# The last chunk's output stores: from GpSimd's queue to the queues of SyncE and ScalarE

## The chip, the cores and the metric

The kernel runs on one core of one Trainium2 chip. The metric is the device time of one execution in microseconds, as the median of several runs. Before the change it is 883.96 us (three runs, 883.19 to 884.87). The profile is one execution, with a span of 881.4 us from its first to its last instruction.

## The reference

A bucketed attention feeds a two-layer block with a squared ReLU:

```python
# q, k, v: (4, 8, 768, 64); proj: (64, 6)
mask   = bucket(q @ proj)[..., :, None] == bucket(k @ proj)[..., None, :]
scores = where(mask, q @ k.T / 8, -1e9)
attn   = softmax(scores)                      # + 1e-9 in the sum
x = (attn @ v).transpose(0, 2, 1, 3).reshape(3072, 512)
h = x @ w_in                                  # (512, 2048)
g = relu(h) ** 2
out = g @ w_out                               # (2048, 512) -> (3072, 512), float32
```

The change concerns only how the last part of `out` leaves the chip.

## The kernel before, in words

The first part, about 0.4 of the span, computes the attention for 16 pairs of heads and keeps the transposed result `x_all` in DRAM. The second part works through the 3072 tokens in three chunks of NCH = 1024. For each chunk it makes the hidden layer (`hidden` for the first chunk, `hidden_pair` for the others) and then projects it (`project(i)`). The products are done with a two-level scheme of seven products instead of eight: `project` goes through seven outer products k = 0 to 6, and each of these is one call of `product`, which does seven inner ones.

`product` (L696) is the piece to know. It makes seven `add`s of four matmuls each (128x256, float32; each shows as two records in the trace), always in the order of factors 0, 1, 4, 3, 5, 6, 2. Adds of factors 0, 4, 5 and 2 go one after another into the same PSUM accumulator `acc0`, and after each of the first three ScalarE takes a snapshot of it (`keep`, L715: the copies `one`, `two`, `three`). The copy has to read the accumulator before the next add changes it, so TensorE waits for `one` before the add of factor 4, for `two` before that of factor 5, and so on. Between adds of `acc0` stand adds into another accumulator, which give the copy time.

Weights come as `leaf` tiles of 256 KB, seven buffers in rotation. Each add calls `a_with_load` (L1136), which issues the load of the leaf five places ahead on ScalarE's queue (`load_leaf`, L988). So ScalarE's instruction stream is a mixture of copies and of leaf loads, in the order of the program.

VectorE combines the products into blocks of the output. A finished block (i, ih, jh) of 128 output columns by 512 tokens goes to `put_out` (L1014): VectorE transposes it within 32x32 squares into a tile `h` (L1018), and four stores write it, one for each group of 32 partitions, a = 0 to 3 (L1025). Each moves 64 KB in runs of 128 bytes. Here ih says which half of the 512 output columns it is, jh which half of the chunk's tokens. Blocks (0,0), (0,1) and (1,0) go out on SyncE's queue (SP), blocks (1,1) on GpSimd's. In the last chunk (i = 2) the first (1,0) block alternates between SP and GpSimd.

Outer product k = 5 (`sixth`, L1097) closes the blocks (0,1) and (1,1), two rows of each; k = 6 (`fourth`, L1105) closes (1,0). The second (1,0) block of the last chunk, the very last output, is handled by `put_last` (L1030): TensorE transposes, ScalarE and VectorE copy one half each (L1040, L1042), and SP and ScalarE store them (L1045).

Each engine carries out its instructions in the order in which the program is built. Stores and loads on ScalarE's queue are issued by ScalarE's sequencer between its copies. After `project` of the last chunk all engines read a flag and pass over a general version of the kernel that is not used for these inputs (L1278, L1279).

The calls around the change are these:

```python
use = uses[k]                     # k = 5: sixth, k = 6: fourth
product(
    NQ, QN, a_with_load, bt, lambda *p: use(0, *p), lambda *p: use(1, *p),
    lambda p: use(2, p, None), lambda *p: use(3, *p), hook,
)
```

so that the blocks of n = 1 (row 0) are closed after the sixth add of a product and those of n = 2 (row 1) after its seventh, and the stores stand at these places of the program, before the first `add` of the next product.

Of the kernel before, what the change touches and what calls it, by code (L numbers as in the profile page):

```python
# [34 lines left out]
def kernel(  # L35
# [10 lines left out]
    nc = tc.nc  # L46
# [20 lines left out]
    NCHUNK = B * S // NCH  # L67
# [516 lines left out]
    with tc.manual_schedule():  # L584
# [21 lines left out]
        for pr in range(NP):  # L606
            a, b = 2 * pr, 2 * pr + 1
# [406 lines left out]
        def put_out(i, ih, jh, n, o):  # L1014


            ot = p_r.tile([P, HN], FP32, name="h", bufs=NH)
            nc.vector.transpose(out=ot, in_=o)  # L1018
            m0 = ih * HD + n * P
            at = slice(i * NCH + jh * HN, i * NCH + (jh + 1) * HN)  # L1020
            for a in range(P // 32):
                queue = nc.gpsimd if (ih, jh) == (1, 1) else nc.sync
                if (i, ih, jh) == (NCHUNK - 1, 1, 0) and a % 2:
                    queue = nc.gpsimd
                queue.dma_start(  # L1025
                    out=out[at, m0 + a * 32:m0 + (a + 1) * 32].rearrange("(c i) j -> i c j", i=32),
                    in_=ot[a * 32:(a + 1) * 32].rearrange("i (c j) -> i c j", j=32),
                )
# [21 lines left out]
        def project(i):  # L1050
# [12 lines left out]
            def close(ih, jh, n):  # L1063
                o = outs[ih, jh, n // 2]
                o[1] += 1
                if (i, ih, jh, n // 2) == (NCHUNK - 1, 1, 0, 1):

                    if o[1] == 2:
                        for col in (1, 0):
                            put_last(n - n % 2 + col, o[0][:, col * QN:(col + 1) * QN])  # L1070
                elif o[1] == 2:
                    put_out(i, ih, jh, n // 2, o[0])
# [407 lines left out]
```

## Time and profile before

| what | value |
|---|---|
| time, median of 3 | 883.96 us (883.19 to 884.87) |
| span of the profiled run | 881.4 us |
| TensorE busy | 866.7 us, 98% |
| VectorE busy | 756.3 us, 86% |
| ScalarE busy | 391.9 us, 44% |
| GpSimd busy | 107.2 us, 12% |
| chain that ended last | 94% TensorE |
| stores of L1025 on SP | 66, of 64 KB |
| stores of L1025 on GpSimd | 26, of 64 KB; 10 of them in the last 20 us |

In the views, PE is TensorE's matmuls and PEld its weight loads, DVE is VectorE, ACT ScalarE, POOL GpSimd and SP SyncE; SPq and ACTq are transfers as the engine's sequencer issues them. A line of the timeline gives the start, the length, the engine, the line of the kernel, the operation, the tile written and the tile read, the count of merged instructions, and in brackets the idle time of the engine before it with what ended it. A line of the chain gives start, length and what the time was spent in. An issue's length is the time on the issuing sequencer and not that of the transfer; the landing times are told apart.

### The profile page before, as it was taken

The numbers are of one execution on the slowest core, as the hardware profiler recorded it, in microseconds if no ns is written. First come the engines' busy times: TensorE is split into PE (matmuls) and PEld (weight loads), VectorE is DVE, ScalarE is ACT, GpSimd is POOL, SyncE is SP. The second block draws the span as 40 slices with busy tenths as digits, with TensorE's granted clock in tenths as the row PEclk, the third lists the DMA queues.
The fourth block names the chain that finished last, engine by engine and source line by source line (L and its number), as shares of the span: only waits on it lengthen the run. The fifth ranks groups of instructions, "written<-read, shape, count | busy, mean of one in ns | idle before, by whom it ended". The sixth has DMA issues, their size and how long they took to land.

```text
span 881.4 us, 12164 instructions
## 1 busy us (share of the span) xinstructions
PE 866.7 (98%) x4364; PEld 519.5 (59%) x4364; DVE 756.3 (86%) x1096; ACT 391.9 (44%) x673; POOL 107.2 (12%) x172
## 2 busy tenths in 40 slices
PE   8999999999999999999999999999999999999996
PEld 3444444444444444444688875556888755568885
DVE  5899999999999998888779978888889788888875
ACT  5988878888888861222211123332111233321110
POOL 2000000000000000564222021111100211110002
PEclk9999999999999999999999999999999999999999
DMA  9678779889677545989897675436847744454565
GB/s 184 123 152 136 196 180 193 178 278 212 148 167 188 156 150 172 322 258 290 282 352 252 181 163 172 159 116 230 291 144 185 174 156 157 129 167 149 162 173 105
DMA packets 224131, 167.09 MB, mean 190 GB/s; under 512 B 164448, under 2 KB 181344, under 8 KB 224064
## 3 DMA queue, kind: packets, MB, share of 16 engines
q1 hardware_dynamic: 189152, 87.19, 41.0%
q0 software_dynamic: 12528, 41.30, 14.9%
q10 hardware_dynamic: 22384, 37.76, 14.1%
q8 instruction: 36, 0.59, 0.3%
q14 instruction: 31, 0.25, 0.1%
HBM read 124.52 MB, written 41.68 MB: 189 GB/s over the span
## 4 chain that ended last, share of the span: by engine, by line
PE 94%; DVE 2%; ACT 1%; DMA 1%; issue 1%; ACTq 0%; DVEq 0%
PE acc L708 40%; PE st L396 17%; PE acc L927 16%; PE xo L438 13%; PE acc L880 5%; PE tot L457 2%; PE hash L346 1%; DVE total L428 1%; DMA k_nat<-in_k_dram 1%; ACT e L413 1%; ACT bits L356 1%; DMA w_in<-s_in 0%; DVE out_piece L179 0%; DVE power L171 0%; ACT small L160 0%
## 5 line engine op out<-in xcount | busy, mean ns | idle before, releaser
L413 ACT ACTIVATE e<-st 128x1024 f32<-128x1024 f32 x192 | 145.1, 810 | 46.9 <-PE st L396 42.7
L396 PE MATMUL st<-feat,feat 64*128 64x512 f32 (+1 forms) x768 | 150.4, 483 | 0.0
L438 PE MATMUL xo<-e,v_nat 128*64 128x512 f32 (+1 forms) x768 | 134.8, 492 | 0.0
L708 PE MATMUL acc<-b,leaf 128*128 128x256 f32 x600 | 133.4, 379 | 0.6 <-issue 0.6
L708 PEld LDWEIGHTS acc<-b,leaf 128*128 128x128 f32 x600 | 113.8, 190 | 17.3 <-issue 2.0
L428 DVE TENSOR_TENSOR total<-total,e 128x1536 f32<-128x1536 f32 x61 | 107.1, 1756 | 4.4
L438 PEld LDWEIGHTS xo<-e,v_nat 128*64 128x64 f32 x768 | 51.4, 136 | 82.4 <-issue 74.9
L927 PE MATMUL acc<-t_x,w_unit 128*128 128x512 f32 x192 | 90.2, 592 | 0.0
L396 PEld LDWEIGHTS st<-feat,feat 64*128 64x128 f32 x768 | 66.0, 188 | 33.5 <-issue 24.1
L708 PE MATMUL acc<-t,leaf 128*128 128x256 f32 x336 | 76.2, 380 | 0.0
L356 ACT ACTIVATE bits<-hash,lifts 32x384 bf16<-32x384 f32 x120 | 68.7, 573 | 3.2 <-issue 1.3
L708 PEld LDWEIGHTS acc<-t,leaf 128*128 128x128 f32 x336 | 63.7, 190 | 9.1 <-DVE t L519 0.5
L792 DVE SCALAR_TENSOR_TENSOR b<-h 128x512 f32<-128x512 f32 x96 | 65.7, 692 | 3.0
L396 PE MATMUL st<-bits,bits 64*128 64x256 bf16 (+1 forms) x384 | 63.0, 325 | 1.8 <-ACT e L413 1.4
L927 PE MATMUL acc<-x,w_unit 128*128 128x512 f32 x128 | 60.1, 592 | 0.0
L708 PE MATMUL acc<-x,w_unit 128*128 128x512 f32 x128 | 56.6, 594 | 0.0
L708 PE MATMUL acc<-b_t,leaf 128*128 128x256 f32 x240 | 53.8, 379 | 0.0
L927 PEld LDWEIGHTS acc<-t_x,w_unit 128*128 128x128 f32 x192 | 36.5, 190 | 28.9 <-issue 26.8
L715 ACT COPY two<-acc 128x256 f32<-128x256 f32 (+1 forms) x29 | 12.5, 432 | 87.7 <-PE acc L708 72.2
L715 ACT COPY one<-acc 128x256 f32<-128x256 f32 (+1 forms) x29 | 12.5, 432 | 85.9 <-PE acc L708 47.6
L708 PEld LDWEIGHTS acc<-b_t,leaf 128*128 128x128 f32 x240 | 45.5, 190 | 6.2
L396 PEld LDWEIGHTS <-bits 64*128 64x128 bf16 x384 | 23.4, 93 | 41.6 <-issue 37.9
(161 smaller groups left out, 1169.7 us busy)
## 6 DMA issues: line engine op xcount, KB each, us to landing
leaf<-w_out ACTq DMA_DIRECT2D x142, 256.0 KB, 3.1
w_unit<-w_in SPq DMA_DIRECT2D x16, 640.0 KB, 3.9
raw<-in_moe_w_in_dram SPq DMA_DIRECT2D x16, 512.0 KB, 5.5
raw<-in_moe_w_out_dram SPq DMA_DIRECT2D x16, 512.0 KB, 4.3
w_unit<-w_in SPq DMA_DIRECT2D x8, 896.0 KB, 7.9
w_out<-sums POOLq DMA_DIRECT2D x16, 448.0 KB, 6.8
sum<-w_in SPq DMA_DIRECT2D x16, 448.0 KB, 4.9
v_nat<-in_v_dram SPq DMA_DIRECT2D x16, 384.0 KB, 4.4
```

Of the source, the lines that this page charges most:

```text
L346: nc.tensor.matmul(out=banks[g * NR_B:(g + 1) * NR_B, h, 0:HS], lhsT=projs[rows], rhs=feat[pr, w][rows, c * HS:(c + 1) * HS], start=True, ...
L356: nc.scalar.activation(out=t[h * D:h * D + NR_B, c * HS:(c + 1) * HS], in_=hashed[pr, w][at, h, 0:HS], func=ACTF.Sign, scale=HUGE, bias=li ...
L396: nc.tensor.matmul(out=st[:, h, 0:hi - lo], lhsT=src[pr, 1][rows, key], rhs=src[pr, 0][rows, lo:hi], start=first, stop=not first,)
L413: nc.scalar.activation(out=e[:, :, lo:hi], in_=sts[i][:, :, 0:hi - lo], func=ACTF.Exp, scale=scale)
L428: nc.vector.tensor_tensor(out=totals[pr], in0=totals[pr], in1=weights[pr, kt][:, :, 0:S], op=ALU.add)
L438: nc.tensor.matmul(out=xo[h * D:(h + 1) * D, lo:hi], lhsT=nat[pr, "v_nat"][:, h, kt * D:(kt + 1) * D], rhs=weights[pr, kt][:, h, lo:hi], s ...
L457: nc.tensor.matmul(out=tot[g * 32:(g + 1) * 32, 0:HS], lhsT=ones, rhs=src[:, h, c * HS:(c + 1) * HS], start=src is srcs[0], stop=src is sr ...
L708: nc.tensor.matmul(out=acc[to], lhsT=a(i), rhs=b(i), start=first and i == 0, stop=last and i == n - 1, skip_group_check=True,)
L715: nc.scalar.copy(out=t, in_=acc[of])
L792: nc.vector.scalar_tensor_tensor(out=out, in0=h, scalar=0.0, in1=h, op0=ALU.max, op1=ALU.mult)
L880: nc.tensor.matmul(out=out, lhsT=w[:, a], rhs=b, start=start, stop=stop, skip_group_check=True)
L927: nc.tensor.matmul(out=acc[to], lhsT=w[:, PLACE[a], f], rhs=bt[b](f), start=first and f == 0, stop=last and f == NFT // 2 - 1, skip_group_ ...
```

## The change

In the last chunk no store is put on GpSimd's queue any more. The blocks of the lower half of the output columns (ih = 1), which are (1,1) and (1,0), alternate between SP and ScalarE: groups a = 0 and 2 on SP, a = 1 and 3 on ScalarE. It is meant to take GpSimd's slower issue out of the end of the kernel and to let two sequencers issue the last stores side by side. Chunks 0 and 1 stay as they were, and so does `put_last`.

```diff
             for a in range(P // 32):
                 queue = nc.gpsimd if (ih, jh) == (1, 1) else nc.sync
-                if (i, ih, jh) == (NCHUNK - 1, 1, 0) and a % 2:
-                    queue = nc.gpsimd
+
+                if i == NCHUNK - 1 and ih == 1:
+                    queue = (nc.sync, nc.scalar)[a % 2]
                 queue.dma_start(
                     out=out[at, m0 + a * 32:m0 + (a + 1) * 32].rearrange("(c i) j -> i c j", i=32),
                     in_=ot[a * 32:(a + 1) * 32].rearrange("i (c j) -> i c j", j=32),
                 )
```

## Prediction

> **What bounds the kernel now.** The page's parts 1 and 4 come first: TensorE is busy 98% of the span, and 94% of the chain that ended last is TensorE. The chain in order of time, cut to the last stretch, shows which engine sets the end, and where it stops doing so.
>
> ```profile
> 860.40 10.38 PE acc L708 x48
> 870.77 0.03 issue
> ...
> 871.79 0.71 DVE h L1018
> 872.50 0.32 DVE tmp L1004
> ...
> 873.32 0.79 PE acc L1035 x4
> 874.11 0.02 issue
> 874.13 0.42 DVE h L1042
> ```
>
> Up to 870.77 matmuls of L708 follow each other without a gap; then come the last sums on VectorE, four transposes, one copy, and the last stores. So in the last product (k = 6, from 860.24) any microsecond that TensorE waits is a microsecond at the end. The timeline of the same stretch shows what it could wait for:
>
> ```profile
> 856.90 1.92 ACTq L994 DMA_DIRECT2D leaf<-w_out  x3
> ...
> 860.24 3.62 PE L708 MATMUL acc<-b_t,leaf 128*128 128x256 f32 x16
> ...
> 860.99 0.71 DVE L1018 STREAM_TRANSPOSE h<-o 128x512 f32<-128x512 f32 x1
> ...
> 862.00 2.62 POOL L1025 DMA_DIRECT2D out_dram<-h  x4 [79.42 <-DVE h L1018]
> ...
> 862.16 0.37 ACT L715 COPY one<-acc 128x256 f32<-128x256 f32 x1 [4.97 <-DMA leaf<-w_out]
> 862.17 0.33 ACTq L994 DMA_DIRECT2D leaf<-w_out  x1
> ...
> 863.69 3.62 PE L708 MATMUL acc<-t,leaf 128*128 128x256 f32 x16
> ...
> 865.15 0.71 DVE L1018 STREAM_TRANSPOSE h<-o 128x512 f32<-128x512 f32 x1
> ```
>
> Sixteen matmuls run from 860.24 (the adds of factors 0 and 1); ScalarE's copy `one` ends at 862.16 + 0.37 = 862.53; the third add starts at 863.69 on the same accumulator, which `one` must have read. The copy has 863.69 − 862.53 = 1.16 us of slack. The two transposes of L1018 make the blocks (1,1) of k = 5. Their stores stand on GpSimd's queue; the second ends at 865.86, well after `one`.
>
> **What the Trainium skill says.** "Perfetto Trace Analysis", section "DMA Instruction — HWDGE (DVE, Sync)": the issuing sequencer itself sits through the semaphore wait and the making of descriptors, and only then is free for its next instruction. The trace agrees as far as it goes: every store of SP waits its turn in order. It has no ScalarE store waiting ahead of a copy, so the blocking there is inferred. "DMA: Bandwidth & Descriptors", section "Issuing engines are not separate DMA queues": all issuers share 16 DMA engines, and a second issuer saves only issue time. Here that saving is small: a store costs GpSimd 0.65 us and SP 0.49 (rows below). "TensorE: Matmul & The Clock Gate", section "What's actually happening": a free-running idle window of about 3.4 us halves TensorE's clock. The trace agrees after the end: in the windows view 878.00 to 879.00 has PEclk 0.56, so the clock fell at 878.12, 4.0 us after the last matmul.
>
> **The change, part by part.** All is in the last of three chunks. Every store writes the same 64 KB as before.
>
> It removes the ten stores on GpSimd, x4, x4 and x2. GpSimd has nothing else to do from 862 on, so this frees nothing that anyone waits for.
>
> It moves four to SP (a = 0 and 2 of the two (1,1) rows). SP only issues transfers; at about 0.5 us each they end before its two L1045 stores at 874.19, so they cost nothing.
>
> It puts six on ScalarE: a = 1 and 3 of the two (1,1) rows and of the one (1,0) row. (Of (1,0), these two were GpSimd's.) The built order on ScalarE becomes:
>
> ```
> three (k=5), leaf, store x2 [waits h of 860.99], leaf, store x2 [waits h of 865.15], leaf, one (k=6), leaf, two, five, three, store x2, h L1040, store L1045 x2
> ```
>
> The first pair waits for 860.99 + 0.71 = 861.70 with only leaf loads behind it. Two are queued before `one`. Those leaves are wanted by the fifth and sixth adds; even at the slowest landing of a store, 7.0 us, they are there if the rest is late too. No cost.
>
> The second pair does the harm. Behind it stand a leaf load and `one`, and TensorE's third add waits for `one`. Step by step:
>
> ```profile
> 860.22 0.32 SPq L1025 DMA_DIRECT2D out_dram<-h  x1
> 860.58 0.49 SPq L1025 DMA_DIRECT2D out_dram<-h  x1
> ...
> L1025 SPq DMA_DIRECT2D out_dram<-h x66: 315/488/882, 492.9 to 872.9; - x66
> L1025 POOL DMA_DIRECT2D out_dram<-h x26: 649/652/678, 506.8 to 873.4; - x26
> ...
> DMA to landing us min/median/max: 1.8/3.0/7.0
> ```
>
> (Single issues on SP, then the view of the tile out_dram.) On SP the first store went out 0.03 after its transpose (859.48 + 0.71 = 860.19, then 860.22), the second 0.36 later, and with its own 0.49 and a 0.04 gap that pair takes 0.89. ScalarE has no such store in this trace; SP is the nearest row. So the pair issues from 865.86 + 0.03 = 865.89 to 866.78. The leaf load takes 0.33 and about 0.06 of semaphore instruction: 867.17. `one` takes 0.37: 867.54. TensorE needs about 0.1 to start: 867.64. It would have started at 863.69, so it loses 3.95, say 4.0 us. From there everything that follows keeps its distances.
>
> Bounds: three back-to-back issues at the shortest 0.32 to 0.33 end at 866.88, so the loss is 866.88 + 0.37 + 0.05 − 863.69 = 3.6. If SP and ScalarE slow each other, as in SP's slowest pair (0.67 from 865.41 to 866.08, then 0.88 + 0.05), the pair takes 1.60, the leaf 0.5, and the loss is 865.89 + 2.10 + 0.47 − 863.69 = 4.8.
>
> The (1,0) pair waits for the transpose that now ends at 872.50, moved by the loss, and issues for 0.89 to 1.60, so to 873.42 or 874.1 (unshifted). Behind it is the copy h L1040, which began at 873.79, and SP's last stores wait for that. So 0 to 0.3 us; I take 0.1.
>
> At the very end I count no gain from GpSimd's absence:
>
> ```profile
> 872.79 1.29 POOL L1025 DMA_DIRECT2D out_dram<-h  x2 [4.06 <-DVE h L1018]
> ...
> 874.59 0.87 ACTq L1045 DMA_DIRECT2D out_dram<-h  x2
> ```
>
> GpSimd's last store starts at 872.79 + 0.64 = 873.43 and lands about 3.3 us later (its queue's median in the DMA view), near 876.7; ScalarE's starts at 874.99 and lands 4.1 later, near 879.1. The second is last. Fewer issuers might save up to 0.5, which I keep for the range only.
>
> Sum: 883.96 + 4.0 + 0.1 = 888.1 us.
>
> **Rivals.**
> A, the forecast: 888.1, with ends 883.96 + 3.6 − 0.5 = 887.1 and 883.96 + 4.8 + 0.3 = 889.1.
>
> B, the stall also drops the clock. An idle of 3.9 us holds a whole free-running 3.4 us window with a chance of about (3.9 − 3.4)/3.4 = 15%, more if the loss is 4.8. Matmuls then run at half speed for 3.4 us or more, which costs 1.7 to 3.4: about 890.6. For it: the fall at 878.12. Against: it took 4.0 us there, and the time is a median of several runs.
>
> C, nothing blocks: the waiting store does not hold the copy behind it, or `one` stays within its slack. Then GpSimd's ten stores go for nothing: 884.0. Against: the built order, and that the second transpose ends 865.86 − 862.16 = 3.7 us after `one` began, thrice the slack.
>
> D, faster: nothing blocks, and the tail did hang on GpSimd's slower issue. Its pair took 1.29, SP's 0.89 or less; taking the pair wholly off gives at most 1.3: 882.7. For it: span end 881.4 is 6 us after the last issue ends at 875.46, so the tail is landings and closing. Against: the landing times above.
>
> **How the numbers follow.** A 0.78, B 0.12, C 0.06, D 0.04. Slower by over 0.2% (above 885.7) is A and B, 0.90; within 0.2% is C, 0.06; faster is D, 0.04. The point is A's, 888.1. The range leaves out C and D (0.10) and the upper part of B. From A's ends, widened by the 0.8 us or so by which the three runs of before differ from their median, and reaching into B: 886.6 to 890.4.
>
> **What would show it.** Right: in the timeline, ScalarE's second pair of L1025 near 865.9, `one` of k = 6 near 867.2 instead of 862.16, and a gap of about 4 us on TensorE before the third add, put down to `one`; the rest moved by the same amount. Clock: PEclk below 1.00 between 863 and 875 would be B. Wrong: `one` still near 862 (C or D), a third add waiting for a leaf instead, stores on ScalarE of over 0.9 us each, or a tail after the last copy that is shorter than before by more than 0.5 us.

## The result, and the profile after

| | before | after |
|---|---|---|
| time, median of 6 runs | 883.62 us (883.19 to 884.87) | 889.75 us (888.62 to 891.18) |
| ratio, 95% interval | | 1.0068 (1.0055 to 1.0081) |
| span of the profiled run | 881.4 us | 886.9 us |
| start of k = 6 on TensorE | 860.24 | 859.73 |
| start of its third add | 863.69 | 867.61 |
| end of TensorE's last matmul | 874.09 | 879.80 |
| from there to the end of the span | 7.35 | 7.06 |

The changed kernel is 6.1 us slower; 888.1 was forecast, with a range from 886.6 to 890.4. Line numbers of the kernel after are one higher than before from L1022 on, so the stores are L1026 and L1046.

The chain of the kernel after, in order of time, around the place where the time is lost (start, length, what it was spent in):

```profile
864.64 0.71 DVE h L1018
865.35 0.03 DVE most L770
865.39 1.81 DMA out_dram<-h
867.20 0.36 ACT one L715
867.56 0.04 issue
867.61 8.88 PE acc L708 x32
...
877.49 0.71 DVE h L1018
...
879.83 0.42 DVE h L1043
```

Before, this stretch was TensorE alone (860.40 to 870.77). Now the chain leaves TensorE: it goes through the second transpose, a store and the copy `one`, and only then back. Note also that 32 matmuls take 8.88 us here, where 48 took 10.38 before. The timeline shows the stations:

```profile
859.73 3.62 PE L708 MATMUL acc<-b_t,leaf 128*128 128x256 f32 x16
...
861.23 0.91 ACTq L1026 DMA_DIRECT2D out_dram<-h  x2
...
862.18 0.52 ACTq L994 DMA_DIRECT2D leaf<-w_out  x1
...
864.64 0.71 DVE L1018 STREAM_TRANSPOSE h<-o 128x512 f32<-128x512 f32 x1
...
865.39 0.86 ACTq L1026 DMA_DIRECT2D out_dram<-h  x2
...
866.37 0.44 ACTq L994 DMA_DIRECT2D leaf<-w_out  x1
867.18 0.37 ACT L715 COPY one<-acc 128x256 f32<-128x256 f32 x1 [10.50 <-DMA out_dram<-h]
...
867.61 5.41 PE L708 MATMUL acc<-t,leaf 128*128 128x256 f32 x16 [4.26 <-ACT one L715]
```

ScalarE's second pair goes out 0.04 us after its transpose, then one leaf load, then `one`, and TensorE stands idle for 4.26 us until `one` has ended. That is the forecast, station by station. The last line holds something more: sixteen matmuls take 5.41 us, where the sixteen before the stall took 3.62. The windows of this stretch (length, TensorE's busy time with its count of matmuls, PEclk, DMA share, GB/s) say why:

```profile
861.73:865.14 3.41, 1.62 (x8) 1.00 0.95 176
865.14:868.55 3.41, 0.94 (x4) 1.00 0.67 111
868.55:871.97 3.42, 3.42 (x9) 0.50 0.89 215
871.97:875.38 3.41, 3.41 (x17) 1.00 0.00 0
```

From 868.55 the granted clock is one half for 3.41 us: 9 matmuls in a window that later holds 17.

So the trace adds up as follows. Without a stall the third add would have begun at 859.73 + (863.69 − 860.24) = 863.18; it began at 867.61, a wait of 4.43. From the third add to the last matmul it is 12.19 instead of 10.40, which is 1.79 at half clock. The tail is 0.29 shorter. 4.43 + 1.79 − 0.29 = 5.93, against 6.1 between the medians. (The two profiled spans differ by 5.4 only, because k = 6 began 0.51 us earlier in the execution profiled after; see what stays open.)

### The profile page after: what moved, and what is told of

Read it like the earlier page. It is cut to its first block, busy times and chain, and to the rows that moved or that the text cites. A ratio compares the mean times of both kernels' runs of the same rounds, so it can differ in the third digit from the quotient of the medians.

```text
span 886.9 us, 12166 instructions
## 1 busy us (share of the span) xinstructions
PE 869.1 (98%) x4364; PEld 521.0 (59%) x4364; DVE 756.2 (85%) x1096; ACT 391.8 (44%) x673; POOL 100.4 (11%) x162
## 4 chain that ended last, share of the span: by engine, by line
PE 94%; DVE 3%; ACT 1%; DMA 1%; issue 1%; DVEq 0%; ACTq 0%
PE acc L708 39%; PE st L396 17%; PE acc L927 15%; PE xo L438 13%; PE acc L880 5%; PE tot L457 2%; PE hash L346 1%; DVE total L428 1%; DMA out_dram<-h 1%; ACT e L413 1%; ACT bits L356 1%; PE xo L326 0%; DVE h L1018 0%; DMA w_in<-s_in 0%; DVE o L1004 0%
## 5 line engine op out<-in xcount | busy, mean ns | idle before, releaser
L708 PE MATMUL acc<-t,leaf 128*128 128x256 f32 x336 | 78.0, 386 | 4.3 <-ACT one L715 4.3
```

The lines of the kernel that those rows point to most:

```text
L708: nc.tensor.matmul(out=acc[to], lhsT=a(i), rhs=b(i), start=first and i == 0, stop=last and i == n - 1, skip_group_check=True,)
```

## Experiments

Theory: the second (1,1) pair on ScalarE, waiting for its transpose, holds `one` back, and the idle time that this makes also drops the clock. Rivals: the delay is due to something else among the moved stores (SP's longer queue, the first pair, the tail), or the clock fell for a reason of its own. All kernels compute the full output; where copies or matmuls are added, they are spare work beside it. "Wait" below is the start of the third add of k = 6 less the start of k = 6 and less the 3.45 us that lie between them before, read from each profile. The diffs are excerpts where a kernel's edit has more lines, such as a flag that limits it to the last k = 6.

**The second pair away from ScalarE.** The kernel after, with these two stores on SP:

```diff
+                if (i, ih, jh, n) == (NCHUNK - 1, 1, 1, 1):
+                    queue = nc.sync
```

> Theory (the second (1,1) pair on ScalarE's queue holds the copy `one` of k = 6, and TensorE idles for it): with this pair on SP and the other four ScalarE stores kept, `one` begins near 862.2 again, TensorE does not idle, the clock stays at 0.998: 883.6 us, give or take 0.7. Rival (six stores on ScalarE's queue cost by their issue and by the traffic in front of the leaf loads, wherever they stand): four of them still cost most of it, 886 to 889.

Measured: 885.73 us (885.15 to 886.6), ratio 1.0021 (1.0011 to 1.0031). The theory's time is missed, and the rival's too, which began at 886; most of the loss is gone. The timeline of this kernel:

```profile
861.80 0.91 ACTq L1028 DMA_DIRECT2D out_dram<-h  x2
862.75 1.00 ACTq L994 DMA_DIRECT2D leaf<-w_out  x2
863.86 0.37 ACT L715 COPY one<-acc 128x256 f32<-128x256 f32 x1 [6.60 <-DMA out_dram<-h]
...
864.28 3.72 PE L708 MATMUL acc<-t,leaf 128*128 128x256 f32 x16 [0.36 <-ACT one L715]
...
873.22 0.89 ACTq L1028 DMA_DIRECT2D out_dram<-h  x2
...
875.12 0.85 SPq L1028 DMA_DIRECT2D out_dram<-h  x2
875.28 0.84 ACTq L1048 DMA_DIRECT2D out_dram<-h  x2
876.07 1.74 SPq L1048 DMA_DIRECT2D out_dram<-h  x2
```

The stall of 4.26 has shrunk to 0.36, and in this profile the clock stays full up to TensorE's last matmul. So the second pair carries the harm. Two smaller losses are left, which the forecast had at nothing. `one` still begins at 863.86 instead of near 862.2: the first pair and two leaf loads stand before it, and the wait is 0.53. And the tail is 8.52 instead of 7.35: SP's stores of 875.12 could have gone with ScalarE's of 873.22, from the same transpose. What they waited for is told by the view of SP's waits in the last 16 us (us in total, times, longest):

```profile
SPq L1028 <- DMA out_dram<-h: 5.1, 3, 4.4
```

They waited for the landing of another store; of the longest, 4.4 us, the part up to 873.19 cost nothing, as the transpose was not done before. A completion semaphore is the counter that tells of a transfer's landing. In the trace the transfers of SP and ScalarE take theirs from the same eight, and SP's store of 875.12 uses the one that ScalarE's store of 873.22 had taken; that store landed at 875.06, and SP's went out 0.06 us later. In the kernel after the order of building gives SP's last stores semaphores whose transfers had landed long before (870.95 and 871.66 for those of 879.90 and 880.29), and its tail shows no such wait.

**The second pair alone.** The kernel before, with only the two ScalarE stores of that row:

```diff
+                if (i, ih, jh, n) == (NCHUNK - 1, 1, 1, 1) and a % 2:
+                    queue = nc.scalar
```

> The kernel before, and only the second (1,1) pair (two stores) moved from GpSimd to ScalarE. Theory: this pair alone gives the whole loss: a gap of about 4.4 us on TensorE before the third add of k = 6, a share of the clock of 0.995, 889.5 us. Rival (the loss is spread over the six stores): a third of it or less, 884 to 886.

Measured: 890.59 us (889.45 to 891.03), ratio 1.0075 (1.0059 to 1.0092). The timeline of this kernel, then its windows:

```profile
866.14 0.90 ACTq L1027 DMA_DIRECT2D out_dram<-h  x2
...
867.16 1.16 ACTq L994 DMA_DIRECT2D leaf<-w_out  x1
...
868.41 0.37 ACT L715 COPY one<-acc 128x256 f32<-128x256 f32 x1 [10.98 <-DMA out_dram<-h]
...
868.84 5.41 PE L708 MATMUL acc<-t,leaf 128*128 128x256 f32 x16 [4.74 <-ACT one L715]
```

```profile
865.63:869.05 3.42, 0.21 (x1) 1.00 0.87 121
869.05:872.46 3.41, 3.41 (x9) 0.50 0.69 197
```

Two stores out of the ten that the change moves make the whole loss, clock included. The wait is 4.91, longer than after, because the leaf load behind the pair took 1.16 us here (0.44 after, 0.33 before). Why was not found. SP was issuing no store at that time; GpSimd was, the row's other two from 866.40 to 867.69, and no run varied that. The pair ahead need not be the reason: of the 142 leaf loads that ScalarE issues in the kernel before, where no store stands ahead of them, the median took 0.33 us and the longest 1.46.

**The second pair later.** The kernel after, with those two stores put into the program behind `two` of k = 6 (a list `late`, emptied there):

```diff
+                if (i, ih, jh, n) == (NCHUNK - 1, 1, 1, 1) and a % 2:
+                    late.append(store)
+                else:
+                    store()
```

> As changed, but the second pair of ScalarE stores stands behind the copy `two` of k = 6 in the order, where ScalarE is idle anyway. Theory: nothing waits behind it, so 883.5 us, clock 0.998, with all ten stores still off GpSimd. Rival (a store on ScalarE costs in itself): over 885.

Measured: 885.57 us (883.72 to 888.93), ratio 1.0018 (1.001 to 1.0026). The timeline of this kernel:

```profile
864.41 3.72 PE L708 MATMUL acc<-t,leaf 128*128 128x256 f32 x16 [0.36 <-ACT one L715]
...
866.57 0.91 ACTq L1031 DMA_DIRECT2D out_dram<-h  x2
```

Same engine, same stores, same bytes; only their place among ScalarE's instructions differs. The wait is 0.53 and the clock full up to the last matmul. So the stall of 4.26 us comes from the order of the stream and not from ScalarE's storing. The time, however, misses the theory's 883.5 and lies where the rival had put it. The profile is of an execution of 884.09 us, one of the faster: it shows 0.62 lost on TensorE up to its last matmul (from the first pair) and a tail of 7.41 (7.35 before). That explains 0.7 of the 1.7 us in the median; for the other 1.0 a cost of the stores themselves is not excluded (see what stays open).

**The clock apart from the wait.** The kernel after, with eight spare matmuls of 128x256 on TensorE ahead of the third add of the last k = 6, into an accumulator that nobody reads (they show as sixteen records):

```diff
+                for _ in range(8):
+                    nc.tensor.matmul(
+                        out=void, lhsT=ident, rhs=bt["11"](0), start=True, stop=True,
```

> As changed, with eight spare matmuls (128x256, into an unused accumulator) put in front of the third add of k = 6, so that TensorE works through about 3.5 us of the wait of 4.4. Theory (the idle time drops TensorE's clock, and this costs 1.8 us beyond the wait): `one` is as late as before, the clock stays at 0.998, 887.9 us. Rival (the slow adds after the wait are from leaves that land late or from something else): 889.7 still.

Measured: 887.9 us (887.36 to 888.44), ratio 1.0046 (1.0029 to 1.0063). The timeline of this kernel, and its windows:

```profile
863.91 3.62 PE L729 MATMUL acc<-b_t,ident 128*128 128x256 f32 x16
...
868.42 3.72 PE L710 MATMUL acc<-t,leaf 128*128 128x256 f32 x16 [0.90 <-ACT one L717]
```

```profile
863.35:866.77 3.42, 3.42 (x18) 1.00 0.83 160
866.77:870.18 3.41, 2.51 (x12) 1.00 0.92 184
```

The wait is as long as after (868.42 − 860.45 − 3.45 = 4.52), but TensorE is idle for only 0.90 of it, and the clock does not fall: sixteen matmuls take 3.72, not 5.41. The time is 1.85 us below that of the kernel after, close to the 1.79 read from the trace (2.06 when each is taken against before in its own comparison).

**Idle time alone.** The kernel before, no store moved, with n spare copies on ScalarE ahead of `one` of k = 6 in the last chunk only:

```diff
+            for _ in range(n):
+                keep(0, "two")
             one = keep(0, "one")
```

> The kernel before (no store on ScalarE's queue but the last two), with 8 spare copies of 0.37 us put in front of `one` of k = 6 on ScalarE. `one` begins 8 x 0.37 = 3.0 us later, of which 1.16 is slack: TensorE idles for 1.8 us. Both theories of the clock (it falls only after a wholly idle window of 3.4 us, or after one that is idle for the most part) see no fall: 885.4 us, clock 0.998.

> The same with 11 spare copies: an idle time of 11 x 0.37 - 1.16 = 2.9 us. If the clock falls only after a wholly idle window of 3.4 us, it never falls: 886.5 us, 0.998. If a window that is idle for the most part is enough (say two thirds, 2.3 us), it falls in many of the runs, by where the window lies: 886.5 without and 888.3 with.

> The same with 14 spare copies: an idle time of 14 x 0.37 - 1.16 = 4.0 us. If a wholly idle window is needed, one run in six sees the fall: 887.6 us mostly, 0.998. If a window idle for the most part is enough, all runs see it: 889.4 us, 0.995.

> The kernel before with 20 spare copies in front of `one` of k = 6 and no store moved. At the 0.28 us that each of the spare copies cost with 8, 11 and 14 of them, TensorE idles for 2.6 + 6 x 0.28 = 4.3 us, as long as in the changed kernel. If the idle time alone makes the loss, with the fall of the clock in every run: 883.6 + 4.3 + 1.8 = 889.7 us, clock 0.995. If the stores add to it by their traffic: 888 or less here. If only a wholly idle window of 3.4 us makes the clock fall, a quarter of the runs has it, and the median is 887.9.

| copies | idle of TensorE in the profile, us | wait, us | time, us | ratio (95%) | clock fell in the profile |
|---|---|---|---|---|---|
| 8 | 0.95 | 1.12 | 884.95 (20 runs) | 1.0016 (1.0009 to 1.0023) | no |
| 11 | 1.78 | 1.94 | 885.7 (7 runs) | 1.0028 (1.0017 to 1.004) | no |
| 14 | 2.61 | 2.78 | 886.42 (5 runs) | 1.0045 (1.003 to 1.0061) | no |
| 20 | 4.27 | 4.43 | 890.14 (4 runs) | 1.0071 (1.0056 to 1.0087) | yes |

A spare copy cost 0.28 us and not the 0.37 of its line, since the next begins before it ends; the waits are shorter than planned for that reason. With 20 copies the wait is 4.43, by chance the very value of the kernel after, and the time is the same within 0.4 us (in the profiled execution half clock lasted two windows and not one). No store is needed for the loss; idle time of TensorE at this place is enough. With 14 copies, three of the five executions had a mean granted clock of 0.997 and took 885.59 to 886.42; two had 0.995 and took 888.15 and 889.77. That fits a fall of the clock in some of them, but no trace of these two was kept. The windows of 11, 14 and 20 copies, one fence each:

```profile
863.54:866.95 3.41, 1.63 (x9) 1.00 0.81 123
866.95:870.36 3.41, 3.41 (x17) 1.00 1.00 199
```

```profile
861.71:865.13 3.42, 1.93 (x9) 1.00 0.74 115
865.13:868.54 3.41, 2.29 (x11) 1.00 0.93 180
868.54:871.95 3.41, 3.41 (x17) 1.00 0.37 70
```

```profile
862.85:866.26 3.41, 1.00 (x5) 1.00 0.78 109
866.26:869.67 3.41, 1.56 (x4) 0.50 0.92 152
869.67:873.09 3.42, 3.42 (x10) 0.50 0.18 64
873.09:876.50 3.41, 3.41 (x18) 1.00 0.00 0
```

The bounds of these windows are laid on the clock's own records: in each of the traces, every change of the clock falls on a grid of 3.413 us, whose start differs from one execution to the next. Take first the windows at full clock. After each in which TensorE was busy for 1.62 us or more (47.5%), the clock stayed full. After each with 32% or less it fell to half; 32% was met in the tails of two other kernels. No window in between was met, so the bound lies somewhere from 32% to 47.5% busy, and a wholly idle window is not needed.

From half clock the record is another. With 20 copies a window 46% busy left it at half. At the start of every kernel the clock is half as well: its record of full speed begins at 4.31 us before and at 6.61 to 6.85 us with the spare matmuls, with 11 copies and with the (1,0) pair alone (below), where the first six transposes take 1.48 to 1.49 us instead of 0.84. In these three a window at half clock 50%, 56% and 57% busy was followed by another at half clock; in before one of 83% was followed by full. Half clock does half the work in the same busy time (9 matmuls against 17). Counted by work, these windows are 23% to 28% and 41%, and one bound between 32% and 41% would fit all of them. That is a reading of these traces that no run tested.

**The parts one by one.** First both pairs later: the kernel after, the first pair behind `one` and the second add of k = 6, the second pair behind `two`:

```diff
+                if (i, ih, jh) == (NCHUNK - 1, 1, 1) and a % 2:
+                    late.append(store)
+                else:
+                    store()
```

> As changed, but both (1,1) pairs of ScalarE stores stand where nothing waits behind them: the first pair behind `one` of k = 6, the second behind `two`. After the first pair turned out to hold `one` by a little too (a gap of 0.36 us on TensorE and `one` at 864.0 instead of 862.2 with the second pair moved behind), the theory is that with both out of the way `one` begins near 862.2, TensorE has no gap, and the time is that of the kernel before, 883.6 us, with at most 0.8 more where SP's last store shares a semaphore with a store issued shortly before it. Rival (stores on the hardware queues slow the last products in another way): 885 or more with no gap before the third add.

Measured: 885.37 us (884.38 to 887.15), ratio 1.002 (1.0013 to 1.0028). The timeline of this kernel:

```profile
863.52 0.37 ACT L715 COPY one<-acc 128x256 f32<-128x256 f32 x1 [4.97 <-DMA out_dram<-h]
...
863.95 0.95 ACTq L1033 DMA_DIRECT2D out_dram<-h  x2
...
865.04 3.62 PE L708 MATMUL acc<-t,leaf 128*128 128x256 f32 x16
```

From the start of k = 6 (861.59) on, TensorE loses nothing any more: no idle time before the third add, and 13.85 us to its last matmul, as before (13.85). Yet the median is 1.6 us above before: the theory's time is missed, and the rival's is met (885 or more with no gap), though its reason, slower last products, does not show in the profile. In the trace, of an execution of 885.26 us, 0.64 is a longer tail, where SP waits for a semaphore as in the first experiment, and 1.35 lies ahead of k = 6, in code that no edit touched.

Then single parts on the kernel before: only the first pair on ScalarE, and only the (1,0) pair on ScalarE instead of GpSimd.

```diff
+                if (i, ih, jh, n) == (NCHUNK - 1, 1, 1, 0) and a % 2:
+                    queue = nc.scalar
```

> The kernel before, and only the first (1,1) pair moved from GpSimd to ScalarE. Theory: its issue ends about 862.7, then two leaf loads of about 0.5 each stand before `one`, which so begins at 863.8 to 864.0; the slack of 1.16 is used up and TensorE waits 0.4 to 0.5: 884.1 us, no fall of the clock. By the prediction's step for this pair (no cost): 883.6.

```diff
                 if (i, ih, jh) == (NCHUNK - 1, 1, 0) and a % 2:
-                    queue = nc.gpsimd
+                    queue = nc.scalar
```

> The kernel before, and only the (1,0) pair of the last chunk moved from GpSimd to ScalarE. Prediction's step: 0 to 0.3 us through the copy h L1040, and at most 0.5 gained at the end: 883.5 us, between 883.1 and 883.9. If the end hung on GpSimd's slower issue: 882.7.

Measured: the first pair 884.31 us (883.65 to 884.91), ratio 1.0005 (0.9996 to 1.0013); the (1,0) pair 883.36 us (882.22 to 884.55), ratio 0.9993 (0.9985 to 1.0002). Neither can be told from before in its time. The traces say a little more. With the first pair alone, this is ScalarE's part of the timeline and what TensorE makes of it:

```profile
863.38 1.02 ACTq L994 DMA_DIRECT2D leaf<-w_out  x2
...
864.50 0.37 ACT L715 COPY one<-acc 128x256 f32<-128x256 f32 x1 [6.62 <-DMA out_dram<-h]
...
864.93 3.72 PE L708 MATMUL acc<-t,leaf 128*128 128x256 f32 x16 [0.38 <-ACT one L715]
```

It is again the loss of about 0.6 on TensorE that the first experiment left over (14.50 instead of 13.85 up to the last matmul). With the (1,0) pair on ScalarE nothing is lost on TensorE, and the tail is 0.22 shorter. That pair is the only ScalarE part of the change whose trace shows no cost; the gain, 0.41 us between the medians, is within the interval of none. No version tried is shown to beat the kernel before.

**What stays open.** The start of k = 6 moves by −0.5 to +1.4 us between profiled executions of different kernels. The −0.5 of the kernel after is there within the first 100 us; the larger shifts (+0.7 with the first pair alone, +1.4 with both pairs later and with 8 copies) arise between 440 and 460 us, in the first chunk's first projections. Before the products of 454.18 TensorE is idle there for 0.34 us in before and for 1.38 with both pairs later, and the profile names no cause ("issue"); nothing there was edited. In the profiled run with both pairs later the shift is what lies above the edits' own costs, and it may be so in that kernel's median and in that of the second pair later (both some 1.0 us above what their traces' edits explain), but a median has no trace. Executions without a kept trace had mean granted clocks down to 0.994 (second pair later) and 0.995 (second pair on SP, both later), against 0.996 to 0.998 of before in the same comparisons, so a fall of the clock somewhere in them, or a cost of the moved stores that no trace shows, is not ruled out. Whether the shift comes with the build or only with the execution was not settled. The varying length of the leaf load behind a pair was not either.

## Why the prediction was right, and where its sizes were not

The measured 889.75 us lies inside the range, but above the upper end, 889.1, of forecast A itself. The range held because it had been stretched towards rival B, which then happened; that is luck as far as A goes. The cause of the stall was foreseen; that the clock would fall with it was given a chance of 0.12.

**The mechanism.** Right at every station. The second pair waits at the head of ScalarE's stream; the leaf load and `one` stand behind it; TensorE's third add waits for `one`. Shown by taking that pair away (stall 0.36), by moving it alone (the whole loss), and by putting it later in the same stream (stall again 0.36, and none with the first pair later too). Rivals C and D are ruled out. The Trainium skill's "Perfetto Trace Analysis", section "DMA Instruction — HWDGE (DVE, Sync)", from which the blocking was inferred, names DVE and SyncE in its title and notes that the mechanism is the same where ScalarE is one of the issuing engines; these runs show it for a store on ScalarE's.

**The wait's size.** The pair: 0.89 forecast, 0.86 measured, so SP was a good row to take. The leaf load and its semaphore instruction were put at 0.33 + 0.06; from the end of the pair (866.25) to the start of `one` (867.18) it is 0.93. That is the term that was too small, by 0.5, and it makes 4.43 instead of 3.95. The load itself is 0.44 of it; nearly as much, 0.37, lies between its end and `one`. The rows of before did hold the warning: single leaf loads there took up to 1.46 us. The upper bound of 4.8 held for this trace; the second pair alone gave 4.91.

**The clock, the step that failed.** Rival B was given 0.12, on the reasoning that a fall needs "a whole free-running 3.4 us window" of idle time and that 3.9 us hold one with a chance of 15%. The Trainium skill's "TensorE: Matmul & The Clock Gate", section "What's actually happening", does speak of one idle window at least. The grid is there, and free-running, as the page says; the condition is milder: at full clock a window only 32% busy was enough. An idle time of 3.95 us, laid anywhere on the grid with equal chance, leaves a window at most that busy in about 80% of the places; that is an estimate from the 32% and the 3.413 us, and it is higher if the bound is. All six executions of the kernel after had a mean granted clock of 0.993 to 0.995; in the profiled ones without a fall in this stretch it was 0.997 to 0.998. The mean alone does not prove a fall, since single executions of other kernels reached 0.994, but in the profiled one the windows show it. The cost, 1.79, is at the low end of the 1.7 to 3.4 that B gave it. So the likeliest case should have been B, near 890, and the measured 889.75 lies between A and B's 890.6 and close to the latter. The evidence of before had a hint: the 4.0 us from the last matmul to the fall at 878.12 was read as time needed. It was the rest of one partly used window, busy for 58%, and then one empty.

**"No cost" of the first pair.** Wrong by 0.6. The step looked at what is queued behind the pair and at who wants those leaves, but not at whether `one`, two leaf loads later, keeps its slack: pair to 862.7, two leaf loads of 0.5 each, and `one` begins at 863.86 (second pair on SP), beyond the 1.16 us of slack. In the kernel after it costs nothing, because the second pair holds `one` far longer; in the variants it is what is left.

**SP's four more stores, and the tail.** In the kernel after they cost nothing, as forecast, and the tail is shorter by 0.29, within the 0.5 allowed for. That is partly luck of the order: in two variants SP waited for completion semaphores that ScalarE's transfers held, and the tail grew by 0.6 to 1.2 us. The forecast had no term for this.

**The sum.** From 888.1: the longer wait adds 0.48, the clock 1.79, the tail and the copy h take off 0.39, and the median of before was 0.34 lower in this comparison than the 883.96 of the start. That gives 889.6, against 889.75.

## What to carry to other kernels

A store put on an engine that also computes is an instruction with a wait in that engine's stream: before moving it, list what stands behind it, and when the data it waits for are ready, against the slack of the first instruction there that another engine needs. On TensorE a stall costs its length, and when it leaves too little work in a 3.41 us window of the clock (32% busy was too little here, 47.5% was enough), about another 1.8 us, or more, for half clock. Here idle times of 4.26 us and more did so in every trace, those of 2.61 us and less in none. If a store must go there, place it behind the copy that the bound engine waits for.

## What the runs showed of the hardware

- In all 13 traces of this study the clock changed only on a grid of 3.413 us, and the change went with TensorE's busy share in the window before: at full clock 47.5% and more kept it full and 32% and less halved it; from half clock 46% to 57% left it half and 83% and more raised it. From this an estimate follows for a single idle time at full clock in otherwise full windows: below about 1.8 us (52.5% of a window) it does not halve the clock, above about 4.6 us (twice 68%) it always does. Between the two the place on the grid decides.
- Half clock lasted one window (3.41 us) when the next window was full of work, and two (6.83 us) when the first of them was itself only 46% busy, with 20 spare copies.
- A pair of 64 KB stores issued by ScalarE took 0.86 to 0.95 us, as on SP (0.89). The leaf load right behind such a pair took 0.44 to 1.16 us. In the kernel before, with no store ahead, the median of the leaf loads is 0.33 us and the longest 1.46.
- A store can wait for the landing of an unrelated store on another queue, through a completion semaphore that both use: 1.9 us for SP's store of 875.12 in the first experiment.
